# A WKV attention with a mixture of experts on one core: four x buffers for tiles 0 to 19, and overflow tokens handled through SyncE

## The chip, the cores and the metric

One core of a Trainium2 chip runs the whole program in one launch. The metric is the device time of one execution in microseconds. In the rows PE is TensorE (PEld its weight loads), DVE is VectorE, ACT is ScalarE, POOL is GpSimd and SP is SyncE; a "q" behind an engine's name marks an instruction of its sequencer (branches, semaphore waits, transfers).

## What is computed

A linear attention with a decaying state, then a top-2 mixture of eight experts over all 3072 tokens, everything in float32:

```python
def _attn_ref(r, k, v, w, u):                       # B, H, S, D = 4, 8, 768, 48
    for t in range(S):
        cur = np.einsum('bhd,bhe->bhde', u[None] * k[:, :, t], v[:, :, t])
        y[:, :, t] = np.einsum('bhd,bhde->bhe', r[:, :, t], state + cur)
        state = w[None, :, :, None] * state + np.einsum('bhd,bhe->bhde', k[:, :, t], v[:, :, t])

def _moe_ref(x, w_gate, w_noise, noise, w1, w2):    # N, D, E, F = 3072, 384, 8, 1024
    noisy_logits = x @ w_gate + np.log1p(np.exp(x @ w_noise)) * noise
    top2 = np.argpartition(-noisy_logits, 2, axis=1)[:, :2]
    top2_l = np.take_along_axis(noisy_logits, top2, axis=1)
    top2_w = np.exp(top2_l - top2_l.max(-1, keepdims=True))
    top2_w /= top2_w.sum(-1, keepdims=True) + 1e-09
    for e in range(E):
        for k in range(2):
            mask = top2[:, k] == e
            h = np.maximum(x[mask] @ w1[e], 0.0)
            out[mask] += top2_w[mask, k, None] * (h @ w2[e])
```

## The kernel before, in words

**First stage, attention (to about 147 us).** The tokens are cut into 24 tiles of 128 (`NT`): tile `i` is time chunk `i // 4` of batch `i % 4`. One pass of the Python loop `for i in range(NT)` writes the instructions of tile `i`; nothing is reordered afterwards, each engine runs its own instructions in the order written, and semaphores join the engines. A pass does, in this order:

- PE transposes r and k of tile `i + 1` (`trans`, L403), and DVE and ACT copy the results out of PSUM (`rT` L408, `kT` L406); DVE reduces `c` (L386) from `rku`.
- PE adds to the state (`kvup`, L431) and multiplies the old state with r (`inter`, into the PSUM tiles `yt`, L456). Every third pass PE also computes gate logits (`logits`, `pl` L512 and L524).
- POOL prepares tile `i + 2`: `kd` (L370) as soon as its `kt` is loaded, then `rku` (L377, L379).
- PE multiplies masked scores with v (`intra`, L468); scores of tile `i + 1` follow (`pa`, L415), and DVE masks them in two halves (`am`, L422).
- PE transposes x of tile `i - 1` for the gate (`xtrans`, L494), then the finished tile back (`back`, `ptb` L477).
- DVE adds `ptb` and ACT's `cv` into the buffer of x (`xout`, L482), and SP stores that buffer into the DRAM tensor `xd` (L486).

`load(i + 4)` stands between these: it puts three transfers (k, r, v of tile `i + 4`, L140) on SP. All transfers of this stage go through SP in the order written, so tile `i`'s store to `xd` stands behind the loads of tile `i + 3`, and in some passes an expert weight load (L321, L324) is between them.

The buffer of x is the part that the change touches. There are two, used in turn, so tile `i` may write its buffer only when tile `i - 2`'s store has landed:

```python
xs = [att.tile([128, XW], F32, name=f"x{j}", bufs=1) for j in range(2)]    # L219, XW = 384 + 8

def xout(i):                                                             # L480
    x = xs[i % 2]
    nc.vector.tensor_add(x[:, :DM]..., PY[i]..., CV[i]...)               # L482
    X[i] = x
    nc.sync.dma_start(xd[i * 128:(i + 1) * 128, :], x)                   # L486
```

The PSUM tile `ptb` that L482 reads shares its bank (tag `py1`) with one of the two `yt` tiles of the next pass, so PE's L456 can go on into that bank only when L482 has read it.

**Second stage, the experts (to 598.6 us).** POOL gathers rows of `xd` by index (L978), PE runs two matrix products per expert with weights split into a high and a low part (`p1`, L1076, and `p2`, L1112), ACT and DVE write the hidden tile `hb` (L1080, L1082), POOL gathers what `out` holds for these tokens (L987), DVE adds (L1129), and POOL scatters the sum back (L1133). `hb` is one buffer of 128 x 6144 float32 in the pool `moe`; it is first written when the first expert's product starts. Each expert has room for a fixed count of tokens (832, 800 or 768 by its place).

**The end.** `tile_counts` wrote into `tab` whether any expert had more tokens than its room, or whether w left the range that the fast attention allows. All engines load this flag (L1424) and branch on it (`tc.If(any_r > 0)`, L1425). Only where it is set does a slow path run: a list of (row, token, gate) is scattered into the DRAM tensor `lst` by 48 indirect transfers of POOL (L1467), and `slow_expert` (L873) loops over each expert's listed tokens beyond its room, with two indirect gathers (L889) and one indirect scatter (L907) of POOL per 128 tokens. In the profiled execution the branch was not taken: no row bears a line of the slow path. Where it is not taken, the engines run a short block of semaphore instructions (they carry L1425), which brings the semaphores to the counts that the slow path would have left, and then the program's last block (its rows carry L1496): SP waits for all transfers, POOL drains, and two barriers close the program.

Of the kernel before, what the change touches and what calls it, by code (L numbers as in the profile page):

```python
# [50 lines left out]
NOT = 4  # L51


@with_exitstack
def kernel(
# [34 lines left out]
    PAD_TOK = 4095  # L90
    LS = 4096
    LT = E * LS
# [23 lines left out]
    lst = dram.tile([LT, 3], I32, name="lst")  # L116
# [102 lines left out]
    xs = [att.tile([128, XW], F32, name=f"x{j}", bufs=1) for j in range(2)]  # L219
    Z = [att.tile([128, NP, 64], F32, name=f"z{b}", bufs=1) for b in range(B)]  # L220
# [3 lines left out]
    tok = const.tile([128, NCH, B], I32, name="tok")  # L224
    row = const.tile([128, NT], I32, name="row")
# [3 lines left out]
    pid = const.tile([1, 2, E], I32, name="pid")  # L229
# [22 lines left out]
    def consts_a():  # L252
# [7 lines left out]
        nc.gpsimd.iota(tok, pattern=[[C, NCH], [S, B]], base=0, channel_multiplier=1)  # L260
        nc.gpsimd.iota(row, pattern=[[128, NT]], base=0, channel_multiplier=1)
# [8 lines left out]
        nc.vector.tensor_copy(pid[:, 1, :], cap)  # L270
# [256 lines left out]

    tok_f = tok.rearrange("p c b -> p (c b)")
# [344 lines left out]
    def slow_expert(e, pool):  # L873
# [5 lines left out]
        ne = nc.values_load(tab[:, ds(e, 1)], min_val=0, max_val=N // 128)  # L879
        c0 = nc.values_load(pid[:, 1, ds(e, 1)], min_val=0, max_val=CAP)  # L880
        with tc.For_i(0, ne, 1) as t:
            li = pool.tile([128, 3], I32, name="s_li")
            nc.sync.dma_start(li, lst[ds(e * LS + c0 + t * 128, 128), :])
            gi = pool.tile([128, 1], I32, name="s_gi")
            nc.vector.tensor_scalar(gi, li[:, 1:2], float(N - 1), None, op0=ALU.min)
            xg = pool.tile([128, XW], F32, name="s_xg")
            pv = pool.tile([128, DM], F32, name="s_pv")
# [3 lines left out]
            p = psum.tile([128, ND, 128], F32, name="s_px", tag="pt", bufs=2)  # L891
            for d in range(ND):
                nc.tensor.transpose(p[:, d, :], xg[:, d * 128:(d + 1) * 128], ident)
            xt = pool.tile([128, ND, 128], F32, name="s_xt")
            nc.vector.tensor_copy(xt, p)
            hT = pool.tile([128, NF, 128], F32, name="s_h")
            for f in range(NF):
                ph = psum.tile([128, 128], F32, name="s_ph", tag="pa", bufs=2)
                for d in range(ND):
                    nc.tensor.matmul(ph, a1[:, d, f * 128:(f + 1) * 128], xt[:, d, :],  # L900
                                     start=(d == 0), stop=(d == ND - 1))
                nc.vector.tensor_scalar(hT[:, f, :], ph, 0.0, None, op0=ALU.max)
            py = psum.tile([128, DM], F32, name="s_py", tag="py0")
            for f in range(NF):
                nc.tensor.matmul(py, hT[:, f, :], a2[:, f, :], start=(f == 0), stop=(f == NF - 1))
# [595 lines left out]
```

## Time and profile before

| what | value |
|---|---|
| median of 3 runs | 608.84 us (605.33 to 3155.98) |
| the profiled execution's own time | 611.11 us |
| its span, first to last instruction | 609.2 us |
| mean granted TensorE clock | 0.989 of full speed |
| busy share of PE, DVE, ACT, POOL | 95%, 60%, 42%, 45% |
| chain that ended last, by engine | PE 83%, DVE 10%, DMA 3%, ACT 2% |

The span leaves out 1.9 us of the execution's own time. The busy share is a mean over both stages. A clock of 1.00 is full speed (2.4 GHz) and 0.50 the lower level (1.2 GHz). The chain is followed back from the last instruction to what released each one; a timeline row gives the start, the length, the engine, the line, the output and inputs and, in square brackets, how long the engine was idle before and who ended that.

### The profile page before, as it was taken

To read this page: it belongs to the slowest core of one execution; us is meant where nothing else is said; L and a number is where in the kernel's file an instruction comes from. 1 tells how busy PE (TensorE), PEld (TensorE's weight loads), DVE (VectorE), ACT (ScalarE), POOL (GpSimd) and SP (SyncE) were. 2 spreads that over 40 slices of the span, in tenths; PEclk is the share of its full clock that TensorE was granted. 3 is DMA by queue.
4 is the path that set the end of the run, shared out by engine and by line. 5 is a ranking of instruction groups with operands and counts; after the bars stand their busy time and mean duration, and the time that the engine had idled before them with its cause. 6 is when DMAs were issued, how large, how long until landed. Compare 5 with 4: busy or idle time off the path is not lost.

```text
span 609.2 us, 12597 instructions
## 1 busy us (share of the span) xinstructions
PE 576.6 (95%) x4502; PEld 539.7 (89%) x4503; DVE 366.0 (60%) x858; ACT 253.0 (42%) x639; POOL 272.0 (45%) x413
## 2 busy tenths in 40 slices
PE   7989998998988899999899999999999999999993
PEld 4878887875977899999899999999999999999992
DVE  9757878996865985654354637464553735455320
ACT  2757777664214232434252434234242534424210
POOL 8767676853024346243424543272445226235201
PEclk9989999999989999999999999999999999999997
DMA  7999886976112428354645656383555538354000
GB/s 133 182 215 223 193 183 132 235 205 184 69 48 68 131 79 223 98 150 127 169 114 159 155 150 173 91 216 109 168 141 154 160 111 207 112 163 118 32 18 30
DMA packets 134233, 85.65 MB, mean 141 GB/s; under 512 B 109729, under 2 KB 124289, under 8 KB 134162
## 3 DMA queue, kind: packets, MB, share of 16 engines
q1 hardware_dynamic: 124434, 56.63, 38.2%
q0 software_dynamic: 9728, 28.14, 15.7%
q8 instruction: 37, 0.61, 0.4%
q14 instruction: 34, 0.28, 0.2%
HBM read 58.33 MB, written 19.51 MB: 128 GB/s over the span
## 4 chain that ended last, share of the span: by engine, by line
PE 83%; DVE 10%; DMA 3%; ACT 2%; issue 1%; POOL 0%; POOLq 0%; DVEq 0%; ACTq 0%
PE ph L1076 33%; PE pym L1112 31%; PE pa L415 3%; PE yt L468 3%; PE pt L403 2%; PE pym L1105 1%; PE pym L1103 1%; PE yt L456 1%; PE ptx L494 1%; DMA xg<-xd,GR 1%; PE pwarm L431 1%; PE ptb L477 1%; DVE am L422 1%; PE pl L512 1%; DVE hb L1082 1%
## 5 line engine op out<-in xcount | busy, mean ns | idle before, releaser
L1112 PE MATMUL pym<-w1h,hb 128*128 128x384 f32 x768 | 200.9, 339 | 1.4 <-issue 1.3
L1112 PEld LDWEIGHTS pym<-w1h,hb 128*128 128x128 f32 x768 | 139.9, 189 | 2.3 <-issue 2.1
L1076 PE MATMUL ph<-xh,w0h 128*128 128x384 f32 (+2 forms) x384 | 133.2, 347 | 0.9 <-ACT xh L1051 0.9
L1076 PE MATMUL ph<-xl,w0h 128*128 128x384 f32 (+2 forms) x384 | 132.7, 346 | 1.1 <-DVE xl L1052 1.1
L1076 PE MATMUL ph<-xh,w0l 128*128 128x384 f32 (+2 forms) x384 | 132.2, 344 | 0.0
L1112 PE MATMUL pym<-w1l,hb 128*128 128x384 f32 x384 | 130.0, 338 | 0.4 <-issue 0.4
L1082 DVE SCALAR_TENSOR_TENSOR hb<-ph,hb 128x384 fp32r<-128x384 f32 x128 | 71.2, 556 | 90.5 <-ACT hb L1080 37.1
L1133 POOL DMA_INDIRECT out_dram<-ot,TK x54 | 54.8, 1015 | 149.5 <-DVE ot L1129 122.7
L1080 ACT ACTIVATE hb<-ph 128x384 fp32r<-128x384 f32 x128 | 63.0, 492 | 108.3 <-PE ph L1076 86.8
L1076 PEld LDWEIGHTS ph<-xh,w0h 128*128 128x128 f32 x384 | 72.1, 188 | 4.4 <-issue 1.7
L1076 PEld LDWEIGHTS ph<-xl,w0h 128*128 128x128 f32 x384 | 72.1, 188 | 2.7 <-DVE xl L1052 1.5
L1076 PEld LDWEIGHTS ph<-xh,w0l 128*128 128x128 f32 x384 | 72.1, 188 | 1.3
L1112 PEld LDWEIGHTS pym<-w1l,hb 128*128 128x128 f32 x384 | 72.6, 189 | 0.6 <-issue 0.5
L978 POOL DMA_INDIRECT xgt<-xd,GR x40 | 41.8, 1044 | 64.3 <-DMA stg<-in_moe_w_dram 19.7
L987 POOL DMA_INDIRECT pv<-out_dram,GA x47 | 52.3, 1113 | 28.0 <-issue 15.5
L1118 ACT ACTIVATE ot<-pym 128x384 f32<-128x384 f32 x39 | 19.2, 491 | 92.2 <-PE pym L1112 64.6
L1052 DVE TENSOR_TENSOR xl<-xq,xh 128x384 fp32r<-128x384 f32 (+2 forms) x40 | 21.3, 532 | 41.9 <-ACT xh L1051 26.8
L397 ACT ACTIVATE cv<-vd,c 128x48 f32<-128x48 f32 x176 | 44.0, 324 | 2.2 <-DVE c L386 2.2
L422 DVE TENSOR_TENSOR am<-pa,mneg 128x512 int32<-128x512 int32 x48 | 32.7, 683 | 14.6 <-PE pa L415 14.4
L370 POOL TENSOR_TENSOR kd<-kt,tabk 128x192 f32<-128x192 f32 x46 | 28.4, 638 | 18.4 <-DMA kt<-in_k_dram 13.5
L1051 ACT ACTIVATE xh<-xq 128x384 fp32r<-128x384 f32 (+2 forms) x40 | 20.0, 500 | 33.8 <-DVE xq L1042 17.6
L1129 DVE SCALAR_TENSOR_TENSOR ot<-ot,GT,pv 128x384 f32<-128x384 f32 (+2 forms) x44 | 26.4, 610 | 11.8 <-ACT ot L1118 11.8
(294 smaller groups left out, 814.9 us busy)
## 6 DMA issues: line engine op xcount, KB each, us to landing
stg<-in_moe_w_dram SPq DMA_DIRECT2D x32, 384.0 KB
stg<-in_moe_w_dram SPq DMA_DIRECT2D x72, 128.0 KB
xq<-xgt SPq DMA_DIRECT2D x172, 36.0 KB
xd<-x SPq DMA_DIRECT2D x24, 196.0 KB
rd<-in_r_dram SPq DMA_DIRECT2D x24, 192.0 KB
vd<-in_v_dram SPq DMA_DIRECT2D x24, 192.0 KB
out_dram<-zrow SPq DMA_DIRECT2D x16, 288.0 KB
kt<-in_k_dram SPq DMA_DIRECT2D x23, 192.0 KB
```

The lines of the kernel that those rows point to most:

```text
L370: (eng or nc.gpsimd).tensor_mul(kd[i % 3][:, h, :D], kt[i][:, h], tabk[:, h, :D])
L397: nc.scalar.activation(CV[i][:, h, :], vt[i][:, h, :], AF.Copy, scale=C8[i][:, h, :])
L422: nc.vector.tensor_tensor(AM[i][:, s].bitcast(I32), PA[i][s].bitcast(I32), mneg.to_broadcast([128, NP, 128]), op=ALU.bitwise_and)
L978: nc.gpsimd.indirect_dma_start(out=xg[:n], out_offset=None, in_=xd[:GROUPS[GEARLY - 1][1] * 128] if early_ else xd, in_offset=bass.Indirec ...
L987: nc.gpsimd.indirect_dma_start(out=pv[:n], out_offset=None, in_=out, in_offset=bass.IndirectOffsetOnAxis(ap=GA[:n, e * NJ + t:e * NJ + t + ...
L1052: nc.vector.tensor_sub(xl[:, g], v, xh[:, g].bitcast(F32))
L1076: nc.tensor.matmul(ph[:, :w_], a[:, d, fs], x[:, :w_ // 32, d], start=(j == 0), stop=(j == len(q) - 1))
L1080: nc.scalar.activation(h_[:, f, 0, :], ph[:, a:b], AF.Relu)
L1082: nc.vector.scalar_tensor_tensor(h_[:, f, 1, :], ph[:, a:b], 0.0, h_[:, f, 0, :].bitcast(F32), op0=ALU.max, op1=ALU.subtract)
L1112: nc.tensor.matmul(py, hb[:, f, a, hs], x[:, f, :], start=(j == 0), stop=(j == len(q) - 1))
L1129: nc.vector.scalar_tensor_tensor(ot[:n], pt[:n], g, PV[e, t][:n], op0=ALU.mult, op1=ALU.add)
L1133: st = nc.gpsimd.indirect_dma_start(out=out, out_offset=bass.IndirectOffsetOnAxis(ap=TK[:n, q:q + 1], axis=0), in_=ot[:n], in_offset=None, ...
```

## The change

Three things change.

1. Tiles 0 to 19 use four buffers of x in turn, tiles 20 to 23 the old two. The two new buffers are columns of `hb`, whose tile is now made at the start; their last eight columns are zeroed by POOL as before.
2. The slow path no longer has the list `lst`, and no transfer of POOL. For an expert with tokens over its room it walks over all 24 tiles of tokens, with plain transfers on SP, and multiplies each tile's result with a gate `gov` that is zero for tokens that are not over. With this the index tensors `tok` and `row` (two POOL instructions at the start) and one DVE copy into `pid` go.
3. `tile_counts` has one more DVE instruction on 8 numbers, which makes the tile count all or nothing.

```diff
-    xs = [att.tile([128, XW], F32, name=f"x{j}", bufs=1) for j in range(2)]
+    xs = [att.tile([128, XW], F32, name=f"x{j}", bufs=1) for j in range(2)]
+    hb = moe.tile([128, NF, 2, 3 * 128], F32R, name="hb", bufs=1)
+    hb = hb.rearrange("p f a b -> p (f a b)").bitcast(F32)
+    xs += [hb[:, j * XW:(j + 1) * XW] for j in range(2)]
...
-        nc.gpsimd.iota(tok, pattern=[[C, NCH], [S, B]], base=0, channel_multiplier=1)
-        nc.gpsimd.iota(row, pattern=[[128, NT]], base=0, channel_multiplier=1)
...
-        nc.vector.tensor_copy(pid[:, 1, :], cap)
...
     def xout(i):
-        x = xs[i % 2]
+        x = xs[i % (4 if i < X_LATE else 2)]
...
+        nc.vector.tensor_scalar(nt, nt, float(NCH), float(NCH), op0=ALU.mult, op1=ALU.min)
...
-    def slow_expert(e, pool):
+    def slow_expert(e, pool, gov):
...
-        with tc.For_i(0, ne, 1) as t:
-            li = pool.tile([128, 3], I32, name="s_li")
-            nc.sync.dma_start(li, lst[ds(e * LS + c0 + t * 128, 128), :])
...
-            for dst, src, ix in ((xg, xd, li[:, 0:1]), (pv, out, gi)):
-                nc.gpsimd.indirect_dma_start(out=dst, out_offset=None, in_=src,
-                                             in_offset=bass.IndirectOffsetOnAxis(ap=ix, axis=0))
...
-            nc.gpsimd.indirect_dma_start(
-                out=out, out_offset=bass.IndirectOffsetOnAxis(ap=li[:, 1:2], axis=0),
-                in_=pv, in_offset=None, bounds_check=N - 1, oob_is_err=False)
+        with tc.For_i(0, nch, 1) as c:
+            for b in range(B):
+                xg = pool.tile([128, DM], F32, name="s_xg")
+                nc.sync.dma_start(xg, xd[ds(c * (B * 128) + b * 128, 128), :DM])
+                pv = pool.tile([128, DM], F32, name="s_pv")
+                nc.sync.dma_start(pv, out[ds(c * 128 + b * S, 128), :])
...
+                nc.vector.scalar_tensor_tensor(pv, py, gc, pv, op0=ALU.mult, op1=ALU.add)
+                nc.sync.dma_start(out[ds(c * 128 + b * S, 128), :], pv)
...
-        ent = slow.tile([128, 2, NT, 3], I32, name="ent")
-        for kk in range(2):
...
-            for i in range(NT):
-                nc.gpsimd.indirect_dma_start(
-                    out=lst, out_offset=bass.IndirectOffsetOnAxis(ap=SLI[:, kk, i:i + 1], axis=0),
-                    in_=ent[:, kk, i, :], in_offset=None)
+        gov = slow.tile([128, E * NT], F32, name="gov")
+        for e in range(E):
+            g = slow.tile([128, 2, NT], F32, name="ge")
...
+            nc.vector.tensor_add(gov[:, e * NT:(e + 1) * NT], g[:, 0], g[:, 1])
```

Outside the slow path every engine keeps its instructions in the old order, apart from the three that go and the three that come; what moves is who waits for what. DVE's instructions around the write of tile 3's x, before (`x_188` is the second of the two buffers, `ptb` the transposed tile; DMAHW5_49 counts the store of tile 1):

```order
L422 TENSOR_TENSOR am<-pa,mneg 128x512 [waits DVE_49,PE_49]
L482 TENSOR_TENSOR x_188<-ptb,cv 128x384 [waits DMAHW5_49,PE_49,Activation_49]
L422 TENSOR_TENSOR am<-pa,mneg 128x512
L408 TENSOR_TENSOR rT<-pt,pwr 128x512 [waits PE_49]
L386 TENSOR_REDUCE c_624<-rku 128x8 [waits Pool_49]
L441 TENSOR_TENSOR zt<-pwarm,z_189 128x192 [waits PE_49]
L442 TENSOR_TENSOR z_189<-zt,w_160 128x4x48 [waits DVE_49,PE_49]
L422 TENSOR_TENSOR am<-pa,mneg 128x512 [waits PE_49]
L482 TENSOR_TENSOR x_187<-ptb,cv 128x384 [waits DMAHW1_49,PE_49,Activation_49]
```

and the same place now (line numbers are some lines lower):

```order
L418 TENSOR_TENSOR am<-pa,mneg 128x512 [waits DVE_49,PE_49]
L478 TENSOR_TENSOR hb<-ptb,cv 128x384 [waits PE_49,Activation_49]
L418 TENSOR_TENSOR am<-pa,mneg 128x512
L404 TENSOR_TENSOR rT<-pt,pwr 128x512 [waits PE_49]
L382 TENSOR_REDUCE c_621<-rku 128x8 [waits Pool_49]
L437 TENSOR_TENSOR zt<-pwarm,z_189 128x192 [waits PE_49]
L438 TENSOR_TENSOR z_189<-zt,w_159 128x4x48 [waits DVE_49,PE_49]
L418 TENSOR_TENSOR am<-pa,mneg 128x512 [waits PE_49]
L478 TENSOR_TENSOR x_186<-ptb,cv 128x384 [waits DMAHW0_49,PE_49,Activation_49]
```

The write of x keeps its place between the two halves of `am`; its wait for a transfer is gone, and the next tile's write (`x_186`, tile 4) now waits for the store of tile 0 (DMAHW0_49).

The last instructions of POOL in the program, before (L881 and L1470 are the ends of the slow path's loops, L1425 the end of the branch, L1496 the last block):

```order
L881 COMPARE_AND_BRANCH
L881 UNCONDITIONAL_BRANCH
L1470 REGISTER_ALU
L1470 COMPARE_AND_BRANCH
L1470 UNCONDITIONAL_BRANCH
L1425 ISA
L1425 UNCONDITIONAL_BRANCH
L1496 ISA
```

and now:

```order
L874 COMPARE_AND_BRANCH
L874 UNCONDITIONAL_BRANCH
L1458 REGISTER_ALU
L1458 COMPARE_AND_BRANCH
L1458 UNCONDITIONAL_BRANCH
L1415 UNCONDITIONAL_BRANCH
L1484 ISA
```

The ISA row of the branch's end is gone; the same instruction stands in the block for the branch not taken, in which it is gone as well.

ACT's instructions around the first write of `hb`, before (L1080; `pl`, `ptm` and `ptx` are PSUM tiles of the gate logits and of transposed x):

```order
L1051 ACTIVATE xh<-ptm 128x384 [waits PE_49]
L515 ACTIVATE ys<-pl 64x128 [waits PE_49,Activation_49]
L525 ACTIVATE lg<-pl 128x32 [waits PE_49]
L1080 ACTIVATE hb<-ph 128x384 [waits PE_49] x8
L1118 ACTIVATE ot<-pym,GT 128x384 [waits DMASW3_49,PE_49]
L1118 ACTIVATE ot<-pym,GT 128x384 [waits DMASW4_49,PE_49]
```

and now (L1070):

```order
L1041 ACTIVATE xh<-ptm 128x384 [waits PE_49]
L511 ACTIVATE ys<-pl 64x128 [waits PE_49,Activation_49]
L521 ACTIVATE lg<-pl 128x32 [waits PE_49]
L1070 ACTIVATE hb<-ph 128x384 [waits DMAHW6_49,DMAHW4_49,DMAHW7_49,PE_49,Pool_49]
L1070 ACTIVATE hb<-ph 128x384 [waits PE_49] x7
L1108 ACTIVATE ot<-pym,GT 128x384 [waits DMASW3_49,PE_49]
L1108 ACTIVATE ot<-pym,GT 128x384 [waits DMASW4_49,PE_49]
```

The first write of `hb` now waits for POOL's zeroing and for three transfer counts, those of the stores of tiles 14, 18 and 19; nothing is moved on this engine. DVE's first write of `hb` (L1082) waits for the last two of them as well.

## Rows read from the trace of the kernel before

**Rows 1.** The profile's page: the span in 40 slices of 15.2 us, in tenths.
```profile
PE   7989998998988899999899999999999999999993
...
PEclk9989999999989999999999999999999999999997
DMA  7999886976112428354645656383555538354000
```

**Rows 2.** Waits from 10 to 150 us: who for whom, total us, times, longest.
```profile
POOL kd L370 <- DMA kt<-in_k_dram: 13.5, 7, 2.8
...
DVE x L482 <- DMA xd<-x: 2.8, 1, 2.8
```

**Rows 3.** Timeline from 22 to 46 us, tiles 3 to 7: start, us, engine, line.
```profile
26.52 0.38 SPq L486 DMA_DIRECT2D xd<-x  x1
...
30.55 0.43 PE L456 MATMUL yt<-rT,z 48*64 48x128 f32 x2
...
31.90 0.56 DVE L482 TENSOR_TENSOR x<-ptb,cv 128x384 f32<-128x384 f32 x1 [2.83 <-DMA xd<-x]
...
32.51 0.77 PE L456 MATMUL yt<-rT,z 48*64 48x128 f32 x14 [1.52 <-DVE x L482]
32.60 1.15 POOL L370 TENSOR_TENSOR kd<-kt,tabk 128x192 f32<-128x192 f32 x2 [2.48 <-DMA kt<-in_k_dram]
...
33.20 1.50 PE L512 MATMUL pl<-xT,wg 128*32 128x128 f32 x18
...
36.71 1.16 PE L415 MATMUL pa<-rT,kT 64*128 64x128 f32 x16
...
39.06 0.60 PE L403 MATMUL pt<-ident,kd 128*128 128x128 f32 x4
...
44.91 2.12 POOL L379 TENSOR_TENSOR rku<-rku,ub 128x192 f32<-128x192 f32 x2
```

**Rows 4.** Timeline of PE, then of DVE, from 50 to 54 us, tile 7.
```profile
50.70 0.67 PE L456 MATMUL yt<-rT,z 48*64 48x128 f32 x16
51.31 0.86 PE L512 MATMUL pl<-xT,wg 128*32 128x128 f32 x18
...
53.35 0.83 PE L415 MATMUL pa<-rT,kT 64*128 64x128 f32 x10
...
51.17 0.54 DVE L386 TENSOR_REDUCE c<-rku 128x8 f32<-128x384 f32 x1
```

**Rows 5.** Windows: us, busy PE, PEld, DVE, ACT, POOL, PEclk, DMA share, GB/s.
```profile
31.00:32.00 1.00, 0.00 (x0) 0.00 (x0) 0.10 (x1) 0.00 (x0) 0.00 (x0) 1.00 1.11 232
...
33.00:34.00 1.00, 1.00 (x18) 0.73 (x15) 1.00 (x3) 0.00 (x0) 1.00 (x3) 0.50 1.08 290
```

**Rows 6.** One tile's, one line's instructions: min/median/max ns, first and last start.
```profile
L1080 ACT ACTIVATE hb<-ph x128: 491/492/513, 151.9 to 586.2; 128x384 fp32r<-128x384 f32 x128
...
L486 SPq DMA_DIRECT2D xd<-x x24: 338/414/1337, 21.4 to 147.7; - x24
```

**Rows 7.** The chain that ended last, in the first 13 us: start, us, what.
```profile
9.48 0.07 DVE pid L270
```

**Rows 8.** Timeline of POOL from 597.9 us: the last row there is.
```profile
599.55 0.99 POOL L1133 DMA_INDIRECT out_dram<-ot,TK  x1 [3.10 <-DVE ot L1129]
```

**Rows 9.** Instructions of line 1425, the branch: min/median/max ns, first and last start.
```profile
L1425 POOLq EVENT_SEMAPHORE  x5: 17/43/2369, 600.4 to 600.7; - x5
...
L1425 POOLq INC_SWDGE_SEM  x1: 1110/1110/1110, 603.1 to 603.1; - x1
```

**Rows 10.** Instructions of line 1496, the last block, same columns.
```profile
L1496 SPq EVENT_SEMAPHORE  x14: 17/28/28, 604.2 to 609.2; - x14
L1496 POOLq EVENT_SEMAPHORE  x4: 17/17/17, 608.1 to 609.1; - x4
L1496 POOLq DRAIN  x3: 50/107/3825, 604.2 to 608.6; - x3
L1496 SPq DRAIN  x3: 7/7/13, 604.9 to 608.3; - x3
```

More of the change, by code (lines that the diff above doesn't have):

```diff
@@ L51 @@
 NOT = 4
+X_LATE = 20
 @with_exitstack
@@ L89 @@
     EARLY = 384
-    PAD_TOK = 4095
     LS = 4096
-    LT = E * LS
     NJ = NM + 1
@@ L115 @@
     xd = dram.tile([N, XW], F32, name="xd")
-    lst = dram.tile([LT, 3], I32, name="lst")
     wp = const.tile([128, NP], F32, name="wp")
@@ L223 @@
     ones_b = const.tile([128, 128], BF16, name="ones_b")
-    tok = const.tile([128, NCH, B], I32, name="tok")
-    row = const.tile([128, NT], I32, name="row")
     ie = const.tile([128, E], F32, name="ie")
@@ L228 @@
     tab = const.tile([1, E + 2], I32, name="tab")
-    pid = const.tile([1, 2, E], I32, name="pid")
+    pid = const.tile([1, 1, E], I32, name="pid")
     cap = const.tile([1, E], F32, name="cap")
@@ L526, in logits_b @@
                              pl[:, 1, :32 * m].rearrange("p (a b) -> p a b", b=32)[:, :, :2 * E], AF.Copy)
-    tok_f = tok.rearrange("p c b -> p (c b)")
     def expneg(a, shape, tg, res, P):
@@ L878, in slow_expert @@
         nc.sync.dma_start(a2, w2[ds(oe, 1)].rearrange("a (c p) f -> p (a c) f", p=128))
-        ne = nc.values_load(tab[:, ds(e, 1)], min_val=0, max_val=N // 128)
-        c0 = nc.values_load(pid[:, 1, ds(e, 1)], min_val=0, max_val=CAP)
-        with tc.For_i(0, ne, 1) as t:
-            li = pool.tile([128, 3], I32, name="s_li")
-            nc.sync.dma_start(li, lst[ds(e * LS + c0 + t * 128, 128), :])
[L884 to L887, printed above, removed]
-            for dst, src, ix in ((xg, xd, li[:, 0:1]), (pv, out, gi)):
-                nc.gpsimd.indirect_dma_start(out=dst, out_offset=None, in_=src,
-                                             in_offset=bass.IndirectOffsetOnAxis(ap=ix, axis=0))
[L891 to L898, printed above, removed]
-                for d in range(ND):
[L900 to L905, printed above, removed]
-            nc.vector.scalar_tensor_tensor(pv, py, li[:, 2:3].bitcast(F32), pv, op0=ALU.mult, op1=ALU.add)
-            nc.gpsimd.indirect_dma_start(
-                out=out, out_offset=bass.IndirectOffsetOnAxis(ap=li[:, 1:2], axis=0),
-                in_=pv, in_offset=None, bounds_check=N - 1, oob_is_err=False)
@@ new lines, in slow_expert @@
+        nch = nc.values_load(tab[:, ds(e, 1)], min_val=0, max_val=NCH)
+        with tc.For_i(0, nch, 1) as c:
[4 more added lines that the diff above has]
+                nc.sync.dma_start(pv, out[ds(c * 128 + b * S, 128), :])
+                gc = pool.tile([128, 1], F32, name="s_gc")
+                nc.vector.tensor_copy(gc, gov[:, ds(e * NT + c * B + b, 1)])
+                p = psum.tile([128, ND, 128], F32, name="s_px", tag="pt", bufs=2)
+                for d in range(ND):
+                    nc.tensor.transpose(p[:, d, :], xg[:, d * 128:(d + 1) * 128], ident)
+                xt = pool.tile([128, ND, 128], F32, name="s_xt")
+                nc.vector.tensor_copy(xt, p)
+                hT = pool.tile([128, NF, 128], F32, name="s_h")
+                for f in range(NF):
+                    ph = psum.tile([128, 128], F32, name="s_ph", tag="pa", bufs=2)
+                    for d in range(ND):
+                        nc.tensor.matmul(ph, a1[:, d, f * 128:(f + 1) * 128], xt[:, d, :],
+                                         start=(d == 0), stop=(d == ND - 1))
+                    nc.vector.tensor_scalar(hT[:, f, :], ph, 0.0, None, op0=ALU.max)
+                py = psum.tile([128, DM], F32, name="s_py", tag="py0")
+                for f in range(NF):
+                    nc.tensor.matmul(py, hT[:, f, :], a2[:, f, :], start=(f == 0), stop=(f == NF - 1))
+                nc.vector.scalar_tensor_tensor(pv, py, gc, pv, op0=ALU.mult, op1=ALU.add)
+                nc.sync.dma_start(out[ds(c * 128 + b * S, 128), :], pv)
@@ L1425 @@
     with tc.If(any_r > 0):
+        thr = slow.tile([128, E], F32, name="thr")
+        for e in range(E):
+            nc.vector.memset(thr[:, e:e + 1], float(CAP if e < 3 else NM * 128 + (TAIL // 2 if e < E - NS else 0)))
         bad_r = nc.values_load(tab[:, E:E + 1], min_val=0, max_val=1)
```

15 lines of the change are left out of this document (6 added, 9 removed).

## The prediction

> **What bounds the kernel now.** I read the page first, then the waits of the first stage, the timeline around the one wait that this change names, the granted clock there, and last what stands behind the last scatter. The page's slices show PE near full in nearly every slice [rows 1]: PE is the bound, and a microsecond is won only where PE stands still, runs at its lower clock, or has finished and the program has not. The reader is to see three places. The first slices have the DMA engines at 7 to 9 tenths, and the clock row has its one 8 in the third slice (30 to 46 us) [rows 1]. Of DVE's writes of x, exactly one waited for a transfer, 2.8 us [rows 2]. And behind the last work there are almost nine microseconds in which only sequencers are active [rows 8 to 10].
>
> **The change part by part: four buffers.** The wait is that of tile 3. Its write could start when tile 1's store had landed; SP issued that store only at 26.52, since loads stood before it, and the write began at 31.90 after 2.83 us of idle DVE [rows 3]. What it cost PE is more than that wait shows. PE had done two of the sixteen L456 products of tile 4 when it ran out of work (30.55 + 0.43), and went on at 32.51, released by this write: 1.52 us idle [rows 3]. Then the clock fell: it stood at 1.00 in the idle microsecond and at 0.50 at 33 to 34 us, that is at 1.2 instead of 2.4 GHz [rows 5]. So the eighteen products of L512 took 1.50 us there and 0.86 us in tile 7, where nothing was late [rows 3, 4]. The whole price is read from these two tiles, which hold the same instructions: from the first L456 to the first L415 it is 36.71 - 30.55 = 6.16 us in tile 4 and 53.35 - 50.70 = 2.65 us in tile 7 [rows 3, 4]. The difference is 3.51 us.
>
> With four buffers tile 3's write waits for no transfer, and those of tiles 4 to 19 wait for a store four tiles back, so SP may be two more tiles behind. Tiles 20 to 23 have the old distance, but no write there waited for a store (the one wait is at tile 3) [rows 2, 3]. DVE was idle for 2.83 us before this write, and every other write that had to wait at all waited only for PE or ACT, so the write can start some 2.5 us earlier, before PE reaches the products that need it.
>
> What is late next is POOL, which waits for SP's loads of k (seven times, 13.5 us in all) [rows 2]. Loads do not come earlier by this change, so the lead of POOL over PE has to cover the 3.5 us. For tile 6, `kd` is ready at 32.60 + 1.15 = 33.75 and PE reads it at 39.06: a lead of 5.3 us. For tile 8, `rku` is ready at 44.91 + 2.12 = 47.03 and DVE reduces it at 51.17: a lead of 4.1 us [rows 3, 4]. Both are over 3.5, so I count the whole of it. Bounds: 0 if something unseen is late right behind it, 1.5 if only the idle goes and the clock falls all the same, 3.5 as counted. Value 3.5, from the like tile.
>
> The new wait: ACT's and DVE's first writes of `hb` now wait for the stores of tiles 14, 18 and 19. Behind them stand the hidden tiles of the first expert, and PE waits for those. But the first `hb` write is at 151.9 us and even tile 23's store was issued at 147.7 [rows 6], so tile 19's, four tiles earlier, has long landed. Cost 0; it would be a landing's few microseconds if the first product moved up by a whole tile and more, which nothing does. At the start DVE loses one copy of 0.07 us that was on the chain [rows 7]; POOL has two memsets for two iotas. The added DVE instruction on 8 numbers in `tile_counts` is behind PE's products. Together 0.1 us or less; I count 0.
>
> **The slow path.** It did not run, so its transfers cost nothing now and cost nothing then. What was executed of it is the block of the branch not taken. There POOL first waits until the last scatter (issued 599.55) has landed: the last of its five semaphore instructions begins at 600.7 and takes 2.37 us, to 603.1. Then comes INC_SWDGE_SEM, 1.11 us, to 604.2, which books the POOL transfers of the path not taken [rows 8, 9]. Only then starts POOL's drain in the last block, 3.83 us, to 608.1, and the barriers take 1.1 us more [rows 10]. With no POOL transfers in the slow path there is nothing to book: POOL branches at about 600.5 and drains at once, beside the landing. If the drain takes the same 3.8 us it ends at 604.3 instead of 608.1: 3.8 us won. SP waits for the landing at 603.1 by itself and needs 0.7 us for its list (604.2 to 604.9) [rows 10], so it is done by 603.9 and hidden.
>
> Bounds: if the drain is short, as the other two of the same block (0.05 and 0.11 us) [rows 10], SP's 603.9 decides, and 4.2 us are won. If the drain cannot begin to count before the scatter has landed, it ends at 603.1 + 3.8 = 606.9, and 1.2 us are won. A loss would need a drain of over 7.6 us, twice the longest row; I put the end at 0. Value 3.8, from the row of the same instruction.
>
> Here the Trainium skill says otherwise: "VectorE: DVE Perf Modes", section "The DRAIN you can't avoid", holds that the drains of a program's pre- and postamble take a constant 12 ns or so on all five engines. By that rule the tail would win 4.2 us, an estimate with the page's figure, and not 3.8. This trace does not agree for POOL: one of its three drains took 3.83 us [rows 10]; SP's took 7 to 13 ns, in line with it.
>
> **The sum.** For the profiled execution 611.11 - 3.5 - 3.8 = 603.8 us. That execution lies 2.3 us above the median of the runs, 608.84; I take the same differences from the median: 601.5 us.
>
> **The rivals.**
> A: the freed PE runs into the loads. Then the first term is given back in small waits for `kd` and `rku` (the 13.5 us of POOL's waits then reach PE), and only the tail wins: 608.84 - 3.8 = 605.0. For it: DMA at 8 to 9 tenths in these slices. Against: the leads above.
> B: the drain counts from the landing. 608.84 - 3.5 - 1.2 = 604.1. For it: the one long drain stands behind the landing; no row shows one beside a transfer in flight.
> C: slower. PE comes 3.5 us closer to POOL at tile 8, where the lead is the smallest, 4.1 us; if loads come just 0.6 us later than in this trace, PE waits there, and each such stop costs like the one removed, since the clock falls behind it. With stops at tiles 8, 10 and 12 it is 3 x 3.5 - 3.5 - 3.8 = +3.2: 612.0. It decides from the third stop on. Against: three stops need leads that shrink, while tile 6 has 5.3 us.
> D: the clock falls without the idle. Then only 1.5 us of the first term go: 608.84 - 1.5 - 3.8 = 603.5. For it: the lower clock came only after PE was busy again. Against: in that slice it came right behind the only empty microsecond.
>
> **How the numbers follow.** Forecast 0.48, A 0.16, B 0.20, D 0.10, C 0.06. The range reaches from the fastest run of before with the largest gains, 605.33 - 3.5 - 4.2, about 597.5, to rival A with three microseconds for the spread of the runs (605.33, 608.84 and the profiled 611.11): 608.0. C is left out. Two per cent of the median, about what a measurement of this kernel can tell from no change, are 12.2 us, and no case reaches that far: faster 0.03, same 0.94, slower 0.03, the outer two for runs that scatter beyond what I saw.
>
> **What would show it right or wrong.** In the new profile DVE's x write of tile 3 should have an idle of about 0.3 us, ended by PE or ACT and not by a store; the third slice of the clock row should be 9; the tile 4 stretch from L456 to L415 should be near 2.7 us; the first expert's first `hb` write should stand about 3.5 us earlier than 151.9. There should be no INC_SWDGE_SEM at the end, and POOL's drain should start near 0.1 us behind the scatter's issue; its length and end tell the forecast (about 3.8 us long) from B (about 6.4). A new clock dip, or waits of PE for `kd` or of DVE for `rku` between 35 and 70 us, would be A or C. The forecast is wrong if the attention stage ends less than 2 us earlier, or if the stretch from the last scatter to the end stays over 8 us.

## The result, and the profile after

The changed kernel takes 601.0 us (median of four runs, 599.99 to 602.94). The kernel before ran four times beside it; one of these runs took 3155.98 us, and the median is 609.5 us with it and 608.84 without it, which is used below. The ratio is 0.9883, with an interval from 0.9833 to 0.9932. So the change wins 0.7 to 1.7%, inside the two per cent that I called no change, and 601.5 us was the forecast. Two later sets of runs gave ratios of 0.9896 (0.9860 to 0.9933) and 0.9924 (0.9894 to 0.9953); they stand with the experiments. Below, a gain in microseconds is the difference of the medians, and behind the ratio its interval is turned into microseconds of the median of before.

The profiled execution took 601.51 us with a span of 599.8 us, where before had 611.11 and 609.2. The spans differ by 9.4 us, and three places make up nearly all of it. The page first (40 slices, now 15.0 us each):

```profile
PE   7999998997989899999999999999999999999995
PEclk9999999999989999999999999999999999999998
DMA  7999986966112428354745656384556537454101
```

Against [rows 1], the third digit of the clock row is 9 instead of 8. The row of before has a second 8, in the twelfth slice, which the prediction passed over when it spoke of "its one 8". It has stayed, and it becomes important below. The last digit of the PE row is 5 instead of 3: less of the last slice is empty.

**The attention stage.** The timeline of the changed kernel around the write that had waited (start, us, engine, line; L478 was L482, L452 was L456, L508 was L512, L411 was L415):

```profile
29.85 0.56 DVE L478 TENSOR_TENSOR hb<-ptb,cv 128x384 f32<-128x384 f32 x1 [0.30 <-ACT xT L492]
...
31.04 0.67 PE L452 MATMUL yt<-rT,z 48*64 48x128 f32 x16
31.64 0.85 PE L508 MATMUL pl<-xT,wg 128*32 128x128 f32 x18
...
33.68 1.16 PE L411 MATMUL pa<-rT,kT 64*128 64x128 f32 x16
```

DVE was idle for 0.30 us before tile 3's write, which ACT released and not a store; all sixteen L452 products run in one piece, L508 takes 0.85 us, and the stretch is 33.68 - 31.04 = 2.64 us where [rows 3] had 6.16. The last product of `back` stands 3.1 us earlier than before, at 142.0 instead of 145.1. These are the rows of that line, of before and then of after (min/median/max ns, first and last start):

```profile
L477 PE MATMUL ptb<-ident,yb x96: 272/273/331, 15.6 to 145.1; 128*128 128x128 f32 x96
```
```profile
L473 PE MATMUL ptb<-ident,yb x96: 272/273/329, 15.1 to 142.0; 128*128 128x128 f32 x96
```

**The expert stage.** A second product of an expert has 72 matmuls, and the chain of the changed kernel shows it as one piece of 12.5 us. In the profile of before the same piece was cut up. The chains, of before and then of after (start, us, what):

```profile
291.54 6.07 PE pym L1112 x35
...
298.14 0.95 issue
299.09 0.34 PE pym L1112
299.43 0.37 issue
...
300.49 6.06 PE pym L1112 x34
306.56 14.61 PE ph L1076 x72
```
```profile
287.68 12.49 PE pym L1102 x72
300.18 14.83 PE ph L1066 x72
```

Before took 306.56 - 291.54 = 15.02 us, after 12.50. These 2.5 us have nothing to do with the change: nothing is edited there, PE waited for no engine, and the clock was 1.00. They came in the execution that the prediction was worked out from and in none of the other profiles (the experiments profile the kernel before once more, without them).

**The end.** The last scatter was issued at 593.57, and these are the rows of the branch and of the last block (same columns as in [rows 9, 10], which they answer; L1415 was L1425, L1484 was L1496):

```profile
L1415 POOLq EVENT_SEMAPHORE  x1: 17/17/17, 594.4 to 594.4; - x1
...
L1484 POOLq EVENT_SEMAPHORE  x4: 17/17/17, 599.0 to 599.7; - x4
L1484 POOLq DRAIN  x3: 50/113/4463, 594.5 to 599.5; - x3
L1484 SPq DRAIN  x3: 7/7/13, 597.6 to 599.2; - x3
```

And this is SP's wait for the last scatter, in the same block, which ends when the scatter has landed (574.4 + 22.6 = 597.0):

```profile
L1484 SPq EVENT_SEMAPHORE  x1: 22617/22617/22617, 574.4 to 574.4; - x1
```

INC_SWDGE_SEM and the wait ahead of it are gone. POOL's drain starts 0.9 us behind the scatter's issue, while the scatter is still in flight, and takes 4.46 us; it ends 1.9 us behind the landing. SP is done at 597.6. From the scatter's issue to the end it is 599.8 - 593.6 = 6.2 us, where [rows 8, 10] had 609.2 - 599.55 = 9.7: 3.5 us won. So the 9.4 us are 3.1 + 2.5 + 3.5 us, and 0.3 in small pieces between.

### The profile page after: what moved, and what is told of

It reads as the page before. It is cut to its first block, busy times and chain, and to the rows that moved or that the text cites. A ratio compares the mean times of both kernels' runs of the same rounds, so it can differ in the third digit from the quotient of the medians.

```text
span 599.8 us, 12595 instructions
## 1 busy us (share of the span) xinstructions
PE 573.6 (96%) x4502; PEld 538.1 (90%) x4503; DVE 365.2 (61%) x858; ACT 252.8 (42%) x639; POOL 272.8 (45%) x413
## 4 chain that ended last, share of the span: by engine, by line
PE 78%; DVE 10%; SPq 3%; DMA 2%; issue 2%; ACT 2%; POOL 2%; POOLq 0%; DVEq 0%; ACTq 0%
PE ph L1066 31%; PE pym L1102 30%; PE pa L411 3%; PE yt L464 3%; PE pt L399 2%; SPq L138 2%; PE ptx L490 1%; PE pym L1095 1%; PE pym L1093 1%; POOL pv L977 1%; PE yt L452 1%; DMA xg<-xd,GR 1%; DVE hb L1072 1%; PE pwarm L427 1%; PE ptb L473 1%
## 5 line engine op out<-in xcount | busy, mean ns | idle before, releaser
L1070 ACT ACTIVATE hb<-ph 128x384 fp32r<-128x384 f32 x128 | 63.0, 492 | 106.9 <-PE ph L1066 84.4
```

The lines of the kernel that those rows point to most:

```text
L1070: nc.scalar.activation(h_[:, f, 0, :], ph[:, a:b], AF.Relu)
```

## The experiments

There are twelve runs, in three sets; each set had its own executions of the kernel before on the same chip. "The tail" is the stretch from the last scatter's issue to the end, "the tile 4 stretch" that from its first product of the old state to its first score product.

**x_only: the buffers alone.** The kernel before, with

```diff
+    hb = moe.tile([128, NF, 2, 3 * 128], F32R, name="hb", bufs=1)
+    hb = hb.rearrange("p f a b -> p (f a b)").bitcast(F32)
+    xs += [hb[:, j * XW:(j + 1) * XW] for j in range(2)]
...
-        x = xs[i % 2]
+        x = xs[i % (4 if i < 20 else 2)]
```

> The kernel before with the four x buffers alone; the slow path keeps its POOL transfers. Theory (the wait of tile 3 cost 3.5 us, the tail is another term): 3.5 us less than before, 605.3 for a median of 608.8; the stretch of tile 4 from the first L456 to the first L415 is about 2.65 us instead of 6.16, the third slice of the clock row is 9, and INC_SWDGE_SEM (1.1 us) and a POOL drain of 3.8 us behind it are still there, some 9.7 us from the last scatter's issue to the end. Rival (what PE wins is lost again at the loads): within 1 us of before, and PE waits for kd or rd between 35 and 150 us. Rival (the whole gain comes from this part, since before's trace shows another 2.3 us of slow products at 297.5 to 300.5 us that the changed kernel's lacks): 6 us less, and that slow stretch is gone here as well.

Measured: 602.64 us against 604.51, a gain of 1.9 us; ratio 0.997 (0.9941 to 0.9998, 0.1 to 3.6 us). In the profile the tile 4 stretch is 33.05 - 30.41 = 2.64 us and the last block is that of before:

```profile
L1428 POOLq INC_SWDGE_SEM  x1: 1110/1110/1110, 595.1 to 595.1; - x1
L1499 POOLq DRAIN  x3: 107/192/3825, 596.2 to 600.9; - x3
```

The stop is gone wherever the buffers are, and the tail is 9.9 us. But the gain by the medians is nearer to 2 us than to 3.5, though its interval reaches from almost nothing to 3.6. The last rival falls: the slow products at 297.5 us were absent here, and 6 us were not won.

**slow_only: the slow path alone.** The changed kernel, with

```diff
-X_LATE = 20
+X_LATE = 0
```

> The changed kernel with two x buffers for all tiles; the slow path is the new one. Theory (the end alone is won): about 3.5 us less than before, 605.3 for a median of 608.8; from the last scatter's issue to the end about 6.2 us instead of 9.7, no INC_SWDGE_SEM, a POOL drain of 3.8 to 4.5 us that starts before the scatter has landed; tile 3's write waits for its transfer as before, the tile 4 stretch is near 6.2 us, and the third slice of the clock row is 8. Rival (the drain ends with the landing whatever stands before it): 1.2 us less.

Measured: 601.02 us against 604.51, a gain of 3.5 us; ratio 0.9958 (0.9929 to 0.9987, 0.8 to 4.3 us). The profile's tail is 6.3 us with a drain of 4.55 us. That bears out the end's size; the rival's 1.2 us lie inside the interval, but not with this tail. But the forecast for the clock was wrong. Timeline and windows of this kernel (windows: us, busy PE, PEld, DVE, ACT, POOL, PEclk, DMA share, GB/s):

```profile
31.22 0.43 PE L452 MATMUL yt<-rT,z 48*64 48x128 f32 x2
...
33.04 0.56 DVE L478 TENSOR_TENSOR x<-ptb,cv 128x384 f32<-128x384 f32 x1 [3.31 <-DMA xd<-x]
33.65 0.66 PE L452 MATMUL yt<-rT,z 48*64 48x128 f32 x14 [2.00 <-DVE x L478]
34.24 0.85 PE L508 MATMUL pl<-xT,wg 128*32 128x128 f32 x18
...
36.28 1.16 PE L411 MATMUL pa<-rT,kT 64*128 64x128 f32 x16
```
```profile
32.00:33.00 1.00, 0.00 (x0) 0.00 (x0) 0.00 (x0) 0.00 (x0) 0.00 (x0) 1.00 0.93 190
...
34.00:35.00 1.00, 1.00 (x28) 0.66 (x21) 1.00 (x3) 0.00 (x0) 1.00 (x3) 1.00 1.13 297
```

PE stood still for 2.00 us, longer than the 1.52 us of [rows 3], and yet the clock stayed at 1.00 and L508 took 0.85 us. The stretch is 5.06 us: the idle alone.

**before_again: the kernel before, unchanged, profiled once more.**

> The kernel before, profiled once more. If the slow products at 297.5 to 300.5 us (PE's instructions 0.70 us apart instead of 0.17, 2.3 us lost) belong to the kernel before, they stand here too, at the same place; if they are a chance of one execution, they are gone and the span is near 607 us. If the step at tile 2 to 3 (x of tile 1 written at 20.55, tile 3's write at 31.90) is the kernel's own, it is here within 0.3 us.

Measured: 602.08 us, span 600.3. The slow products are gone (the 72 matmuls take 12.48 us), and here too the stop came without a fall of the clock:

```profile
30.54 0.43 PE L456 MATMUL yt<-rT,z 48*64 48x128 f32 x2
...
31.37 0.56 DVE L482 TENSOR_TENSOR x<-ptb,cv 128x384 f32<-128x384 f32 x1 [2.31 <-DMA xd<-x]
31.98 0.66 PE L456 MATMUL yt<-rT,z 48*64 48x128 f32 x14 [1.01 <-DVE x L482]
32.57 0.86 PE L512 MATMUL pl<-xT,wg 128*32 128x128 f32 x18
...
34.62 1.16 PE L415 MATMUL pa<-rT,kT 64*128 64x128 f32 x16
```

The stretch is 4.08 us. So the same program lost 3.5 us at this place in one execution and 1.4 in another.

**warm4: work for PE while it waits.** The kernel before, with

```diff
+                    if i == 4 and (q, j, s) == (0, 0, 0):
+                        for _ in range(10):
+                            nc.tensor.matmul(pwarm[:, 192:], wsrc[:, :128], wsrc[:, :320], start=True, stop=True)
```

> The kernel before (two x buffers, the wait of tile 3 stays) with ten more products of a zero operand, 128 x 320 in bf16, for PE behind the first L456 product of tile 4, where PE stands still for 1.52 us; their result is not used. Theory (the clock falls because PE stood still): PE waits the same 1.5 us, but with products to do, the granted clock stays at 1.00 at 33 to 34 us, and the tile 4 stretch is about 4.2 us instead of 6.16, so some 2 us less than before. Rival D of the prediction (the clock falls whether PE stands still or not): the clock is 0.50 again behind the wait, the stretch stays near 6.2 us, no gain or a loss up to the 1.4 us of the added products.

Measured: 604.01 us against 604.51, ratio 0.9992 (0.9964 to 1.0021). It doesn't answer its question: in the profiled execution tile 1's store had landed in time, tile 3's write was released by ACT, and no wait was there to fill. The ten products then cost their own 1.53 us. That too is a finding: the wait itself comes and goes between executions.

**after_again: the changed kernel beside before on a second chip.** No edit.

> The changed kernel once more, beside the kernel before on this chip, where that has a median of 604.5 us instead of 608.8. By the prediction's two terms (3.5 + 3.8) it should be at 597.2 us. By what the profiles of the first experiments show (the tail wins 3.6 us in every one, but the stop at tile 4 is 1.3 to 2.3 us without a fall of the clock in two of three executions) it should be at 604.5 - 3.6 - 1.8 = 599.1 us. If the two parts' single gains (1.9 and 3.5 us by the medians) simply add, also 599.1. Granted clock: one fall somewhere behind a stop between 140 and 185 us or none, none at 33 to 36 us.

Measured: 598.7 us against 605.86, a gain of 7.2 us; ratio 0.9896 (0.9860 to 0.9933, 4.1 to 8.5 us). The median is nearer to the 599.1 us of the second sum than to the 597.2 of the prediction's terms, but the interval holds both. The single times run from 596.29 to 601.25. The profiled one was the fastest: no fall of the clock while PE had work, tail 6.4 us.

**pool3 and pool12: what the drain waits for.** The changed kernel, with five or twenty of these behind the last scatter:

```diff
+    for _ in range(5):
+        nc.gpsimd.tensor_mul(ub[:, :4].rearrange("p h d -> p (h d)"), ub[:, :4].rearrange("p h d -> p (h d)"),
+                             ub[:, 4:].rearrange("p h d -> p (h d)"))
```

> The changed kernel with five multiplications of 128 x 192 on POOL (0.6 us each by the rows of such an operation) behind the last scatter and ahead of the branch, on a table that nothing reads again; POOL's drain starts some 3 us later, when the scatter has just landed. Theory (the drain has a length of its own): it takes 3.83 us again, as in every execution of the kernel before, and the stretch from the last scatter's issue to the end grows by 2.3 to 3 us, from 6.2 to about 8.9 us. Rival (the drain is a wait that ends some 1.9 us behind the landing): it takes about 1.5 us and the stretch stays at 6.2 to 6.5 us.

> The same with twenty multiplications, some 12 us, so that POOL's drain starts long after the scatter has landed. Theory (a length of its own): 3.83 us again, and the stretch from the last scatter's issue to the end is 1.0 + 12 + 0.4 + 3.83 + 0.8, about 18 us. Rival (the drain waits for something that the last POOL transfers leave to be done): it is short, 0.1 us, and the stretch is about 14.3 us.

Measured: 599.75 us and 612.02 us. POOL's rows of pool3, then of pool12 (the scatter and the added work from the timeline, the drain from the rows of its line):

```profile
588.55 0.98 POOL L1123 DMA_INDIRECT out_dram<-ot,TK  x1 [3.14 <-DVE ot L1119]
589.55 3.27 POOL L1411 TENSOR_TENSOR ub<-ub 128x192 f32<-128x192 f32 x5
...
L1488 POOLq DRAIN  x3: 50/107/3825, 593.3 to 597.7; - x3
```
```profile
590.82 0.98 POOL L1123 DMA_INDIRECT out_dram<-ot,TK  x1 [3.14 <-DVE ot L1119]
591.82 13.27 POOL L1411 TENSOR_TENSOR ub<-ub 128x192 f32<-128x192 f32 x20
...
L1488 POOLq DRAIN  x3: 50/107/3825, 605.6 to 610.0; - x3
```

The tails are 9.5 and 19.5 us, where about 8.9 and 18 were expected; the added work took 3.27 and 13.27 us. The drain is 3825 ns in both, to the nanosecond the length of [rows 10], although it began 14.8 us behind the scatter in the second. So behind a landing it has a fixed length. That is half of the answer. In the eight profiles in which the drain began before the scatter had landed, its end follows the landing. Times in us from the last scatter's issue; the landing is the end of SP's wait for the scatter and, in the row "before", the end of POOL's wait for it:

| profile | landed | drain from, to | drain's length | from landing to drain's end |
|---|---|---|---|---|
| changed kernel | 3.44 | 0.88, 5.35 | 4.46 | 1.91 |
| three | 3.53 | 0.91, 5.44 | 4.54 | 1.91 |
| after_again | 3.65 | 0.91, 5.57 | 4.66 | 1.91 |
| after_third | 4.03 | 0.91, 5.94 | 5.03 | 1.91 |
| one_dma (below) | 4.28 | 2.06, 6.19 | 4.14 | 1.91 |
| before | 3.51 | 4.70, 8.52 | 3.83 | 5.01 |
| pool3 | 3.71 | 4.79, 8.62 | 3.83 | 4.90 |
| pool12 | 4.29 | 14.79, 18.62 | 3.83 | 14.33 |

fills, slow_only and one_buf have 1.91 us in the last column as well. So in all fourteen profiles the drain ends at the later of two times, 3.825 us behind its own start or 1.91 us behind the landing, and no profile is off by more than 1 ns. The rival's "some 1.9 us behind the landing" holds for the changed kernel, and the theory's 3.83 us for pool3, pool12 and the code of before. In pool3 POOL's own instructions set the end; in the changed kernel the landing does.

**one_buf: more of the same stops.** The changed kernel, with

```diff
-        x = xs[i % (4 if i < X_LATE else 2)]
+        x = xs[0 if i < 12 else i % 2]
```

> The changed kernel with one x buffer for tiles 0 to 11, two after that: each of the writes of tiles 1 to 11 must wait until the store of the tile ahead of it has landed (some 4.5 to 5.5 us behind its issue), so the stop of tile 4 comes some ten times. The first theory (each stop of PE is followed by the lower clock and costs 3.5 us in all): the granted clock is 0.50 behind most of the stops, its mean between 20 and 75 us below 0.8. Rival (a stop is its idle time alone, and the clock falls behind few of them): the clock stays at 1.00 behind most stops, and each costs only what DVE's write was late.

Measured: 603.12 us, one run. Both expectations assumed ten stops, and there was one: tile 1's write waited 4.86 us, PE stood still for 3.83 us, and after that no write waited for a store any more. Timeline and windows:

```profile
24.81 0.56 DVE L478 TENSOR_TENSOR x<-ptb,cv 128x384 f32<-128x384 f32 x1 [4.86 <-DMA xd<-x]
...
26.11 1.12 PE L464 MATMUL yt<-am,vd 128*64 128x128 f32 x8 [3.83 <-DVE am L418]
27.16 2.08 PE L411 MATMUL pa<-rT,kT 64*128 64x128 f32 x16
```
```profile
22.00:24.00 2.00, 0.28 (x6) 0.03 (x2) 0.00 (x0) 0.41 (x2) 2.00 (x4) 1.00 1.04 244
24.00:26.00 2.00, 0.00 (x0) 0.00 (x0) 1.19 (x3) 0.00 (x0) 2.00 (x5) 0.54 1.04 211
26.00:28.00 2.00, 1.89 (x16) 1.59 (x18) 1.29 (x3) 0.73 (x4) 2.00 (x5) 0.50 0.98 160
```

One stop delays all later writes, but hardly SP's stores: SP issued tile 2's store at 31.60, 0.02 us behind its write, where the changed kernel issued it at 30.93, 4.8 us behind. So the stores had time to land, and the wait came a single time. In this long stop the clock did fall: L411 takes 2.08 us instead of 1.16.

**three: is the distance of four needed?** The changed kernel, with

```diff
-        x = xs[i % (4 if i < X_LATE else 2)]
+        x = xs[i % (3 if i < 18 else 2)]
```

> The changed kernel with three x buffers for tiles 0 to 17 instead of four for tiles 0 to 19. Theory (only the wait for tile 1's store was late; with three buffers tile 3's write needs the store of tile 0, issued near 21.5 us): no write of x waits for a transfer, no stop of PE at tile 4, and the time is that of the changed kernel within its spread. Rival (the gain needs SP to fall two tiles behind): writes wait again for their stores in tiles 3 to 6, and about 3 us of the gain are lost.

Measured: 598.67 us against 602.70, ratio 0.9937 (0.9913 to 0.9961); the changed kernel in the same set has 0.9924. No write of x waited for a store, and the tile 4 stretch is 32.94 - 30.30 = 2.64 us. Three buffers do what four do, as far as these runs tell them apart: only tile 1's store was late.

**one_dma: what INC_SWDGE_SEM costs.** The changed kernel, with one POOL transfer in the path that is not taken:

```diff
+        lone = slow.tile([128, XW], F32, name="lone")
+        nc.gpsimd.indirect_dma_start(out=lone, out_offset=None, in_=xd,
+                                     in_offset=bass.IndirectOffsetOnAxis(ap=GR[:, 0:1], axis=0))
```

> The changed kernel with one transfer of POOL (an indirect load that is read by nothing) in the slow path, which does not run. Theory (any POOL transfer in the path not taken makes POOL wait for the last landing and book it): INC_SWDGE_SEM is back with about 1.1 us behind a wait of about 2.4 us, the drain of 3.83 us starts behind it, and the stretch from the last scatter's issue to the end is 9.7 to 10 us as in the kernel before. Rival (the price grows with the number of transfers, which was about 51 in the code of before): INC_SWDGE_SEM takes some 0.05 us, the stretch is below 9 us.

Measured: 598.51 us, one run; the tail is 7.0 us.

```profile
L1415 POOLq EVENT_SEMAPHORE  x1: 17/17/17, 590.6 to 590.6; - x1
L1415 POOLq INC_SWDGE_SEM  x1: 1093/1093/1093, 590.7 to 590.7; - x1
...
L1487 POOLq DRAIN  x3: 50/107/4137, 591.8 to 596.5; - x3
```

Half of each theory holds. INC_SWDGE_SEM is back with 1.09 us for one transfer, against 1.11 us for the code of before, so its price hardly grows with their number. But POOL didn't wait ahead of it: the long semaphore wait of [rows 9] (2.37 us) did not come back with a single transfer. The tail is 0.7 us longer than the 6.3 us of three and of fills, and the table above shows why: the scatter landed at 4.28 us instead of 3.53 and 3.57, and the drain ended 1.9 us behind it. A landing as late as 4.29 us stands in pool12 too, which has no INC_SWDGE_SEM. The drain's own 3.83 us would have ended at 2.055 + 3.825 = 5.88, ahead of the 6.19 measured, so in this execution the 1.09 us cost nothing. Behind a landing at 3.5 us they would cost about 0.4 us, an estimate from the same rows (5.88 against 3.53 + 1.91 = 5.44). With one transfer the tail is 2.8 us shorter than the 9.8 us of the old code, so most of the tail's gain is POOL's wait and not the bookkeeping.

**fills and after_third: is it the stops that let the clock fall?** The thirteen profiles without added work in these places share two long stops (from one matmul's start to the next): 1.5 to 1.7 us near 145 us, where the first expert's second matmul waits for `xl`, and 2.7 to 3.0 us near 172 us, where transposes wait for a gather. A fall of the clock stands behind the first in three of them and behind the second in four, in no profile behind both. fills is the changed kernel with zero products in both (`spin(n)` issues n products of 128 x 192):

```diff
+                if fine and f == 0 and j == 0:
+                    spin(14)
...
+            if "x01" not in did:
+                did.add("x01")
+                spin(24)
             next(x01, None)
```

> The changed kernel with products of a zero operand (128 x 192 in bf16, their result not used) in two of the stops that all profiles share: 14 behind the first product of the first expert (stop of 1.7 us near 144 us) and 24 ahead of the transposes that wait for the gather of the first expert's second chunk (stop of 2.7 to 2.9 us near 172 us). In ten profiles the granted clock fell to 0.50 behind the first stop in three and behind the second in three. Theory (a stop of PE is what lets the clock fall): no fall behind either stop, the time is that of the executions without a fall, about 597.5 us where the changed kernel has 598.7, and no execution is over 600. Rival (the clock falls as often with PE busy): falls remain in more than half of the executions, and the time is that of the changed kernel or up to 2 us above it.

> The changed kernel a third time, as the measure for the other kernels of this set: 0.989 of the kernel before, 598 to 600 us, POOL's drain 4.4 to 4.9 us long beside the scatter's transfer, 6.2 to 6.6 us from the last scatter's issue to the end.

Measured, against 602.70 us of before in this set:

| kernel | median, us | lowest to highest, us | runs | ratio |
|---|---|---|---|---|
| changed kernel (after_third) | 598.16 | 596.14 to 600.34 | 7 | 0.9924 (0.9894 to 0.9953) |
| three | 598.67 | 596.26 to 601.68 | 12 | 0.9937 (0.9913 to 0.9961) |
| fills | 596.69 | 596.32 to 596.96 | 6 | 0.9904 (0.9881 to 0.9927) |

The fastest executions are equal, but fills has no slower ones: its six times lie within 0.64 us, where the changed kernel and its like spread over 4 to 5. What a fall costs at the second stop is seen from one_dma, whose clock fell there, and after_third, whose didn't. Their windows, one_dma's first:

```profile
174.00:176.00 2.00, 2.00 (x10) 1.90 (x9) 0.50 (x1) 0.19 (x1) 0.41 (x1) 0.55 0.50 134
176.00:178.00 2.00, 2.00 (x9) 1.97 (x8) 0.56 (x1) 0.30 (x1) 0.00 (x0) 0.60 0.16 13
```
```profile
174.00:176.00 2.00, 2.00 (x15) 1.97 (x14) 0.80 (x2) 0.50 (x2) 0.45 (x1) 1.00 0.52 134
176.00:178.00 2.00, 1.25 (x10) 0.90 (x8) 0.84 (x2) 1.04 (x3) 0.00 (x0) 1.00 0.20 14
```

At 0.55 PE has ten matmuls in two microseconds, at 1.00 fifteen. And this is PE's timeline of fills at that place:

```profile
170.71 2.15 PE L164 MATMUL pwarm<-zrow 128*128 128x192 bf16 x24
173.39 0.55 PE L1043 MATMUL ptm<-ident,xg 128*128 128x128 f32 x3 [0.53 <-DMA xg<-xd,GR]
```

The zero products take 2.15 us of the wait, 0.53 us of it is left, and the useful work goes on when the gather has landed, as before. fills has the lowest median of all kernels that ran here. It is 1.5 us below that of the changed kernel; the intervals of the two ratios overlap, so it is the spread, and not the median alone, that speaks for the theory. The mean granted clock, on record for every execution, says the same: it is 0.996 to 0.998 in all six of fills, and below 0.996 in twelve of this set's nineteen executions of the changed kernel and of the kernel with three buffers. Of the profiled executions with the new slow path and no added work on POOL, the four without a fall have 0.997 or 0.998 and the four with one 0.991 to 0.995. The rival would need six executions in a row without a fall; at seven in nineteen that comes by chance about once in 400 times, an estimate from these counts.

## Why the prediction was right, and where it was not

**The sum.** Forecast 601.5 us and 7.3 us won; measured 601.0 us, and 7.8, 7.2 and 4.5 us won by the medians of the three sets that hold both kernels. The third set's interval, 2.8 to 6.4 us, leaves 7.3 out. So the places are as predicted, and that the time came out within 0.5 us is in part luck: the first term is as large as in one execution and too large for the typical one, and the base of 608.84 was the median of only three runs, far apart. At the first place the mechanism is as predicted but for the clock; at the second another event than forecast sets the end.

**T1, four buffers: 3.5 us predicted.** The step that failed is the last of "the whole price is read from these two tiles", together with "I take the same differences from the median". The tile 4 stretch shrank from 6.16 to 2.64 us, 3.52 us, exactly the term. But of the 3.5 us only the idle belongs to the program, and not even that in every execution. In the four profiles with two buffers the stretch was longer than 2.64 us by 3.52 (before), 1.44 (before_again), 2.42 (slow_only) and, without a wait, by nothing beyond the added products and 0.3 us (warm4: 4.46 - 1.53 - 2.64). The mean is 1.9 us, and the buffers alone gained 1.9 us (0.1 to 3.6; that interval by itself does not exclude 3.5). The clock fell behind one of the three stops at this place. The trace that the prediction read held a warning: PE's two stops of 1.5 us near 148 and 152 us, from one product's start to the next, have no fall behind them. The bound of 1.5 us, "if only the idle goes", was nearer to the typical execution than the value I took.

Rival D had the right amount for T1 with the wrong reason. It said that the clock falls without the idle; in the profiles without the stop the clock at 33 to 36 us was 1.00 in every one. The truth lies the other way round: the idle comes without a fall in two cases of three.

**T2, the end: 3.8 us predicted, 3.5 measured.** The tail was 9.69, 10.09, 9.90 and 9.63 us in the four profiles with the old slow path, 6.19 to 6.78 us in those of the changed kernel and of slow_only, three and fills. The drain does start beside the landing, as forecast. What failed is the step "If the drain takes the same 3.8 us", with the landing hidden behind it: the drain would have ended 4.7 us behind the scatter's issue and ended at 5.35, because its end came 1.9 us behind the landing. Rival B was right that the landing sets the end and wrong in the length, 3.8 us instead of 1.9. That the term came out 0.3 us from its value is in part luck: 3.83 us behind the start and 1.9 us behind the landing lie near each other here.

Here the Trainium skill's rule that I had weighed, "VectorE: DVE Perf Modes", section "The DRAIN you can't avoid" (some 12 ns for the drains of the pre- and postamble on every engine), cannot be carried over to POOL's drain in this program's last block: the runs show 3825 ns and more, and SP's 7 to 13 ns beside it.

**The rest.** The leads of POOL were enough: it waited for k ten times instead of seven (14.0 us in all, 13.5 before), but between 22 and 60 us PE has a single idle piece in the new timeline, 0.42 us for ACT, and none for a load, so rivals A and C fell. Its two waits for r, 0.84 us at 10.6 and 0.97 us at 21.0 us, lie ahead of the place that the change frees. The new waits of `hb` cost nothing. What I had not counted is the 2.5 us of slow products in the profile of before, which made the difference of the two profiled executions, 9.4 us in the spans, look larger than what the change gives.

## What to carry to other kernels

A price read from one execution has two parts: the wait, which the program makes, and what the clock does behind it, which differed here between executions of the same program; count the first in full and the second by how often it is seen in several executions. Where PE must wait for more than a microsecond anyway, products that nobody reads cost nothing there if they fit into the wait, and they made the times of this kernel steadier, and by the medians lower. A path that is not taken is not free while it holds transfers of POOL: look at what stands between the last transfer and the end of the program. No run here took the path, so what the new one costs when it is taken is not known.

## What the runs showed of the hardware that I had not expected

- The same stop of PE has different consequences. Behind the stop of 2.7 to 3.0 us near 172 us the granted clock fell to 0.50 in four of thirteen profiles. The Trainium skill, "TensorE: Matmul & The Clock Gate", section "HAM oscillation — how this bites in real kernels", tells of a kernel in which a wait for data lets the clock fall at every pass; here the trace agrees that such falls stand behind waits, and not that they come each time; the page's waits, some 3 to 5 us, are longer than these.
- POOL's drain in the last block took 3825 ns in each of the six profiles in which the last scatter had landed before it began. In the other eight it took 4.14 to 5.03 us and ended 1.91 us behind the landing.
- INC_SWDGE_SEM took 1.09 us for one transfer in the path not taken and 1.11 us for the code of before. Why POOL waits for the last landing with the many transfers and not with the single one, which was a load and not a scatter, was not tried.
- In one execution PE's products started 0.70 to 1.39 us apart for about 3 us (297.7 to 300.5 us of the profile of before), instead of 0.17, at a granted clock of 1.00, with "issue" as the only reason that the chain names. It happened in no other profile, and its cause stays open.
